# Induced attention and a maxout layer on one core: the first phase's loads, steps and score banks put in another order, and other slots' maxout sums kept in PSUM

## The chip, the core and the metric

The kernel runs on one core of a Trainium2 chip (trn2). Time is device microseconds of one execution, lower is better. The profile is of one execution; its engines are PE (TensorE, matmuls; PEld is its weight load), DVE (VectorE), ACT (ScalarE), POOL (GpSimd) and SP (SyncE, which issues the DMAs). Each engine works through its own queue strictly in the order in which the program wrote it, and waits there on semaphores of the others.

## The reference

Four batches of 12544 tokens with 128 channels first attend from 32 inducing vectors to the tokens (`h`), then from the tokens to `h`; the result goes through a maxout layer of width 768.

```python
def mab(q, kv):
    s = scale * (q @ kv.transpose(0, 2, 1))
    a = np.exp(s - s.max(-1, keepdims=True))
    a /= a.sum(-1, keepdims=True) + 1e-09
    return a @ kv
h = mab(I, x)
y = mab(x, h)                       # 50176 tokens x 128
m = np.maximum(np.maximum(y @ w1, y @ w2), y @ w3)
return (m @ w_out).astype(np.float32)
```

The weights arrive as float64. x is read in float32.

## The kernel before

**Tiling.** A batch has 98 tiles of 128 tokens: group 0 has 2 tiles ("short"), groups 1 to 6 have 16. A full group is four chunks of 512 columns, so a batch has 25 chunks. A chunk needs six slots, one for each 128 of the 768 hidden units: 600 slots in all. A full group's 24 slots are called a window; in this text (b, g) is the window of batch b and group g, and slot k of it is k = 0 to 23.

**First phase** (`phase1_first`, L511, run by the string `STEPS1`). Batch 0's attention from the inducing vectors, and the conversion of the float64 weights, stand in one hand-written order of short steps. `T g.k` transposes four tiles of group g on PE into one of four PSUM banks, `c g.k` copies them out on ACT. `S g` multiplies them with the inducing vectors on PE (into bank `aux0` or `aux1` by turns), `M` takes the maximum on DVE, `D` and `G` spread it over the partitions (ACT, PE), `L` takes the least over the parts (DVE), `E` is the exponential on ACT, `R` a transpose on DVE, `U` the product with the tokens on PE into one bank, `H` the copy of that product to SBUF (ACT). `K` adds the groups up (POOL for groups 0 to 3, DVE for 4 and 5; group 6 is added by `hs`). `W k` is the next step of the conversion of weight k (0 w2, 1 w_out, 2 w1, 3 w3): six operations over 768 columns on DVE, of which the fifth, an addition, is on POOL for w1 and w3, then for w1 one and for w3 two subtractions of w2; `z` is the square of a weight's high half on ACT, which the sixth operation reads. `F n` issues n matmuls whose result nobody reads. `rec`, `hT` form `h` at the end; from there on the first chunks start.

**Loads.** `first_loads` issues the DMAs of the groups of batch 0 (0 to 6) and of the four weights (7 w2, 8 w_out, 9 w1, 10 w3) on SP in the order of `LOADS`.

**The slots** (`advance`, L808, and `stage2`, L889). Step s of the main loop issues for slot s+1 the matmul `pu` (L819) and its Relu on ACT (`ru`, L834), for slot s the matmul `pv` (L825) and the maximum `h = max(pv, ru)` on DVE (L852), for slot s-1 the rounding `hi` of h on ACT (L841) and the rest `lo = h - hi`, on POOL (L849) or, where `low` says so, on DVE at the end of the next step (L855), and for slot s-6 the three matmuls that add hi and lo times w_out into the chunk's bank `acc` (L898). `pu` and `pv` have two banks each, so `pv` of slot s+2 waits for the maximum of slot s. [...] `acc` alternates between two banks (`bank_o`); the one not in use is called `spare`.

**The turns.** Beside the slots, the plan of the main loop puts the attention of the batches 1 to 3 from the inducing vectors into the windows, one group ("turn", L1012 on) at a time: at slot 2 of a window three blocks of matmuls for it, two slots later its maximum (DVE, L407), then two exchanges of partial maxima between partitions by small copies on POOL (`turn_swap`, L429: two copies issued in step 5 and four in step 9), each followed by a reduction on DVE (L437: to `mq` in step 8, to `mm` in step 11), and the exponential. Windows (0,1) to (0,3) have a second such place at slot 14. Windows (2,5), (2,6) and those of batch 3 have no turn. The scores of the next group against `h` are worked on in steps 3 to 15 of a window (DVE L742 to L776).

**Which slots' `lo` is on DVE before.** In batch 3 the slots 0, 5, 14, 18, 21. In (0,1), (0,2) and in group 5 of the other batches 4, 16, 18, 21, all with h in SBUF; in group 6 the same four, 18 and 21 with h in `aux1`; in all other windows 4, 15, 18, 21, the last three with h in `aux1`. So slot 4 of each window of batches 0 to 2 is on DVE, with h in SBUF.

Of the kernel before, what the change touches and what calls it, by code (L numbers as in the profile page):

```python
# [8 lines left out]
F32 = mybir.dt.float32  # L9
# [16 lines left out]
def kernel(ctx, tc, x, xt, ind_t, w1, w2, w3, w_out, out):  # L26
    nc = tc.nc
    B, N, C = x.shape
    M = ind_t.shape[1]
    DF = w1.shape[1]  # L30
    P = 128
    NT = N // P
    NJ = DF // P
# [4 lines left out]
    OB = 2  # L38
    MANUAL = {mybir.EngineType.PE, mybir.EngineType.Activation, mybir.EngineType.SP, mybir.EngineType.DVE, mybir.EngineType.Pool}

    LOADS = (0, 7, 1, 2, 8, 3, 4, 9, 5, 10, 6)
    GROUPS = (0, 1, 2, 3, 4, 5, 6)
    STEPS1 = (
# [8 lines left out]
    )  # L52

    TC = 4
    ORDER = "a a b a a b a b 0 w l a b a a b b 1 2 a b p c b P s X 3 Y S z s s s s s b s"
    STEPS2 = (3, 6, 7, 8, 9, 10, 11, 12, 14, 15)
    scale = 1.0 / float(C) ** 0.5
    LOWVEC = (4, 16, 18, 21)
    LOWBANK = (4, 15, 18, 21)
    LOWLAST = (0, 5, 14, 18, 21)  # L60
    OUTVEC = (0, 2)
    UW = 2 * DF + C
# [3 lines left out]
    groups = []  # L66
    t0 = 0
    while t0 < NT:
        nt = NT % GT if t0 == 0 and NT % GT else GT
# [4 lines left out]
    NG = len(groups)  # L74
# [43 lines left out]
    xts_free = [const.tile([P, GT * P], F32, name=f"xT{i}", tag=f"xT{i}") for i in range(XTB)]  # L118
    xgs_free = [const.tile([P, GT, C], F32, name=f"xg{i}", tag=f"xg{i}") for i in range(XB)]
    w_space = xts_free.pop()  # L120
    shelf = const.tile([P, UW + 2 * groups[0]["nt"] * P + 2 * P + 2 * M + OB * 512 + groups[0]["nt"] * C], F32, name="shelf")
    shelf_at = [0]

    def place(n):
        shelf_at[0] += n
        return shelf[:, shelf_at[0] - n : shelf_at[0]]
# [2 lines left out]
    short_t = [place(groups[0]["nt"] * P) for i in range(2)]  # L129
    short_x = place(groups[0]["nt"] * C).rearrange("p (t c) -> p t c", c=C)  # L130
    iT = place(M)

    def load_raw(src):
        r = bp.tile([P, 2 * DF], U32, name="raw", tag="raw", bufs=4)
# [115 lines left out]
    def start_batch(b):  # L250
        st = state[b] = {"xT": {}, "xg": {}, "a": {}, "s": {}}
        if b == 0:
            st["lst"] = bp.tile([P, NG], F32, name="lst", tag="lst", bufs=1)
            st["mneg"] = bp.tile([P, NG], F32, name="mneg", tag="mneg", bufs=1)
            st["hg"] = outs[1].rearrange("p (g c) -> p g c", c=C)
        else:
            st["mm"] = bp.tile([P, NK], F32, name="mm", tag="mm")
            st["fac"] = bp.tile([P, NK], F32, name="fac", tag="fac")
            st["hs"] = bp.tile([P, C + 1], F32, name="hs", tag="hs")

    def load_tokens(b, k):
        for gi in turns[k]:
# [28 lines left out]
    def attend_products(b, gi, bank):  # L291
        w = groups[gi]["nt"] * M
        st = state[b]
        xT = st["xT"][gi]
        sp = bank
        for q in range(NQ):
            nc.tensor.matmul(
                out=sp[q * M : (q + 1) * M, :w], lhsT=iT, rhs=xT[:, q * w : (q + 1) * w], start=True, stop=True
            )
        st["a"][gi] = sp  # L300
# [210 lines left out]
    def phase1_first():  # L511

        start_batch(0)
        nc.sync.dma_start(out=iT, in_=ind_t)
        nc.scalar.mul(out=iT, in_=iT, mul=scale)
        first_loads()
        st = state[0]
        weights = [convert(k) for k in range(4)]

        groupwise = {  # L520
            "S": lambda gi: attend_products(0, gi, bank_a[GROUPS.index(gi) % 2]),
            "M": lambda gi: attend_max(0, gi),
            "D": lambda gi: attend_column(0, gi),
            "G": lambda gi: attend_spread(0, bank_o[0]),
            "L": lambda gi: attend_least(0, gi),
            "E": lambda gi: attend_weights(0, gi),
            "R": lambda gi: attend_transpose(0, gi),
            "U": lambda gi: attend_sums(0, gi, bank_u[1] if gi == GROUPS[-1] else bank_o[1]),
            "H": lambda gi: attend_keep(0, gi),
            "K": lambda gi: add_group(st, gi),  # L530
            "W": lambda k: next(weights[k], None),
            "z": measure,
            "F": unread_products,
        }
        once = {
            "w2T": transpose_w2,
            "w2h": copy_w2,
            "woh": lambda: nc.scalar.copy(out=wo_hi, in_=wo),
            "least": lambda: combine_least(st),
            "wts": lambda: combine_weights(st),  # L540
            "lw": lambda: sum_groups(st),
            "fac": lambda: last_factor(st),
            "tl": lambda: last_sum(st),
            "tot": lambda: total_sums(st, bank_o[0]),
            "rec": lambda: invert_total(st),
            "hs": lambda: add_last(st),
            "selw": lambda: last_mask(st),
            "pa": lambda: combine_groups(st, "hs", st["selw"], bank_u[0]),
            "sum": lambda: combine_groups(st, "hb", sel[:, :M], bank_u[0]),
            "hT": lambda: combine_states(st, NQ),  # L550
        }
        for step in STEPS1.split():
            if step in once:
                once[step]()
            elif step[0] in "Tc":
                gi, k = step[1:].split(".")
                (transpose_x if step[0] == "T" else copy_x)(0, int(gi), int(k))
            else:
                groupwise[step[0]](int(step[1:]))
        xts_free.append(w_space)  # L560
        start_batch(1)
        load_channels(1, 0)

# [248 lines left out]
    def advance():  # L812

        s = pipe["next"]
        pipe["next"] += 1
        if s + 1 < len(slots):
            c, j = slots[s + 1]
            pu, w = bank_u[(s + 1) % 2], c.w
            nc.tensor.matmul(  # L819
                out=pu[:, :w], lhsT=state[c.b]["us"][:, 2 * j * P : (2 * j + 1) * P], rhs=c.pT[:, :w], start=True, stop=True  # L820
            )
        if 0 <= s < len(slots):
            d, j = slots[s]
            pv = bank_v[s % 2]
            nc.tensor.matmul(  # L825
                out=pv[:, : d.w],
                lhsT=state[d.b]["us"][:, (2 * j + 1) * P : (2 * j + 2) * P],
                rhs=d.pT[:, : d.w],
                start=True,
                stop=True,  # L830
            )
        if s + 1 < len(slots):
            ru = hp.tile([P, 512], F32, name="ru", tag="ru", bufs=3)
            nc.scalar.activation(out=ru[:, :w], in_=pu[:, :w], func=AF.Relu)  # L834
            relus[s + 1] = ru
        low = pipe.pop("low", None)
        if 0 <= s - 1 < len(slots):
            c, j = slots[s - 1]
            h = sums.pop(s - 1)
            hi = hp.tile([P, 512], F32R, name="hi", tag="hi", bufs=9)  # L840
            nc.scalar.copy(out=hi[:, : c.w], in_=h[:, : c.w])  # L841
            lo = hp.tile([P, 512], F32R, name="lo", tag="lo", bufs=10)
            c.hh.append(hi)
            c.hl.append(lo)
            args = dict(out=lo[:, : c.w], in0=h[:, : c.w], in1=hi.bitcast(F32)[:, : c.w])
            if c.low(j):
                pipe["low"] = args
            else:
                nc.gpsimd.tensor_sub(**args)  # L849
        if 0 <= s < len(slots):  # L850
            h = bank_a[1] if d.in_bank(slots[s][1]) else hp.tile([P, 512], F32, name="h", tag="h", bufs=5)
            nc.vector.tensor_max(out=h[:, : d.w], in0=pv[:, : d.w], in1=relus.pop(s)[:, : d.w])  # L852
            sums[s] = h
        if low:
            nc.vector.tensor_sub(**low)  # L855

    class Chunk:
# [8 lines left out]
                self.key = "B" if q else "A"  # L866
                self.base = 0 if q is None else groups[0]["nt"] if q == 0 else (q - 1) * TC

        def low(self, k):

            if self.q is None:
                return False
            if self.b + 1 == B:
                return NJ * self.q + k in LOWLAST
            return NJ * self.q + k in (LOWVEC if self.first_free() > min(LOWBANK[1:]) else LOWBANK)

        def first_free(self):

            if self.b + 1 == B:
                return 0  # L880
            if self.gi == NG - 2 or self.b == 0 and self.gi < 3:
                return WIN
            return 18 if self.gi == NG - 1 else 13

        def in_bank(self, k):

            return self.low(k) and NJ * self.q + k >= self.first_free()

    def stage2(c, j):  # L889
        us = state[c.b]["us"]  # L890
# [260 lines left out]
```

## Time and profile before

| | |
|---|---|
| time, median of 3 runs | 818.93 us (818.26 to 819.09) |
| the profiled execution | 818.5 us |
| its span in the profile | 816.7 us |
| PE busy in the span | 806.1 us (99%) |
| DVE, ACT, POOL busy | 654.7, 719.2, 661.1 us |
| granted TensorE clock | 1.00 |

The page has the busy time of each engine, the span in slices, the DMA queues, the chain of work that ended last, and the costliest groups of instructions by line of the kernel. In rows of the timeline the first two numbers are the start and the duration in us; "x8" is a number of merged instructions, and a bracket at the end of a row tells how long the engine had been idle and what ended it. In rows of groups, "busy us, mean ns" stand behind the count. In rows of waits stand the waiting line, what it waited for, the total in us, the number of waits and the longest.

### The profile page before, as it was taken

The numbers are of one execution on the slowest core, as the hardware profiler recorded it, in microseconds if no ns is written. First come the engines' busy times: TensorE is split into PE (matmuls) and PEld (weight loads), VectorE is DVE, ScalarE is ACT, GpSimd is POOL, SyncE is SP. The second block draws the span as 40 slices with busy tenths as digits, with TensorE's granted clock in tenths as the row PEclk, the third lists the DMA queues.
The fourth block names the chain that finished last, engine by engine and source line by source line (L and its number), as shares of the span: only waits on it lengthen the run. The fifth ranks groups of instructions, "written<-read, shape, count | busy, mean of one in ns | idle before, by whom it ended". The sixth has DMA issues, their size and how long they took to land.

```text
span 816.7 us, 15025 instructions
## 1 busy us (share of the span) xinstructions
PE 806.1 (99%) x4565; PEld 628.3 (77%) x4565; DVE 654.7 (80%) x1198; ACT 719.2 (88%) x1446; POOL 661.1 (81%) x640
## 2 busy tenths in 40 slices
PE   8999999999999999999999999999999999999998
PEld 5667778777787787777777777877778778777886
DVE  6889778787796797887987978878789878878874
ACT  6779889898898898988988989989889999999996
POOL 0369898798798987977988889889878888878886
PEclk9999999999999999999999999999999999999999
DMA  9334643543553335335453353344232222222221
GB/s 344 140 149 141 212 148 106 183 125 105 157 173 123 126 112 175 125 106 177 130 159 117 110 175 120 110 127 126 59 98 66 84 65 78 69 81 74 62 79 51
DMA packets 45408, 101.47 MB, mean 124 GB/s; under 512 B 9360, under 2 KB 15376, under 8 KB 40208
## 3 DMA queue, kind: packets, MB, share of 16 engines
q1 hardware_dynamic: 45184, 100.39, 38.6%
q8 instruction: 36, 0.59, 0.3%
q14 instruction: 44, 0.36, 0.1%
q10 hardware_dynamic: 144, 0.13, 0.0%
HBM read 48.12 MB, written 25.69 MB: 90 GB/s over the span
## 4 chain that ended last, share of the span: by engine, by line
PE 92%; DVE 3%; DMA 2%; ACT 1%; issue 1%; POOL 0%; SPq 0%; DVEq 0%; ACTq 0%
PE acc L898 49%; PE pv L825 16%; PE pu L819 16%; PE aux L707 3%; PE acc L894 3%; PE acc L485 2%; PE aux L388 2%; DMA raw<-in_w_dram 2%; DMA xg<-in_x_dram 1%; POOL rest L207 0%; DVE h L852 0%; ACT ru L834 0%; PE aux L669 0%; DVE mx L745 0%; ACT hi L841 0%
## 5 line engine op out<-in xcount | busy, mean ns | idle before, releaser
L849 POOL TENSOR_TENSOR lo<-h,hi 128x512 fp32r<-128x512 f32 (+1 forms) x498 | 626.6, 1288 | 107.3 <-ACT hi L841 61.8
L852 DVE TENSOR_TENSOR h<-pv,ru 128x512 f32<-128x512 f32 (+1 forms) x534 | 356.2, 672 | 129.6 <-PE pv L825 100.7
L834 ACT ACTIVATE ru<-pu 128x512 f32<-128x512 f32 (+1 forms) x600 | 367.6, 613 | 66.5 <-PE pu L819 62.1
L841 ACT CAST hi<-h 128x512 fp32r<-128x512 f32 (+1 forms) x534 | 333.5, 625 | 4.7 <-DVE h L852 3.6
L898 PE MATMUL acc<-hi,wo_hi 128*128 128x512 f32 (+1 forms) x601 | 235.0, 391 | 0.0
L825 PE MATMUL pv<-pT,us 128*128 128x512 f32 (+1 forms) x600 | 232.7, 388 | 1.6 <-DVE h L852 1.4
L819 PE MATMUL pu<-pT,us 128*128 128x512 f32 (+1 forms) x600 | 231.9, 387 | 0.1
L898 PE MATMUL acc<-hi,wo_lo 128*128 128x512 f32 (+1 forms) x601 | 231.5, 385 | 0.0
L898 PE MATMUL acc<-lo,wo_hi 128*128 128x512 f32 (+1 forms) x601 | 231.3, 385 | 0.0
L898 PEld LDWEIGHTS acc<-hi,wo_hi 128*128 128x128 f32 x601 | 112.8, 188 | 41.5 <-issue 20.5
L825 PEld LDWEIGHTS pv<-pT,us 128*128 128x128 f32 x600 | 112.6, 188 | 29.3 <-DVE h L852 5.4
L819 PEld LDWEIGHTS pu<-pT,us 128*128 128x128 f32 x600 | 112.6, 188 | 24.6 <-ACT ru L834 1.7
L898 PEld LDWEIGHTS acc<-lo,wo_hi 128*128 128x128 f32 x601 | 112.8, 188 | 23.0
L898 PEld LDWEIGHTS acc<-hi,wo_lo 128*128 128x128 f32 x601 | 112.9, 188 | 21.8
L852 DVE TENSOR_TENSOR aux<-pv,ru 128x512 f32<-128x512 f32 x66 | 45.9, 695 | 11.8 <-PE pv L825 5.3
L855 DVE TENSOR_TENSOR lo<-aux,hi 128x512 fp32r<-128x512 f32 x66 | 45.2, 686 | 0.8 <-PE acc L898 0.8
L841 ACT CAST hi<-aux 128x512 fp32r<-128x512 f32 x66 | 41.3, 626 | 0.1
L910 ACT COPY shelf<-acc 128x512 f32<-128x512 f32 (+1 forms) x65 | 39.3, 604 | 0.0
L894 PE MATMUL acc<-pT,us 128*128 128x512 f32 (+1 forms) x100 | 38.8, 388 | 0.0
L855 DVE TENSOR_TENSOR lo<-h,hi 128x512 fp32r<-128x512 f32 x36 | 30.0, 833 | 0.4 <-PE acc L898 0.2
L207 POOL TENSOR_TENSOR rest<-rest,t 128x768 f32<-128x768 f32 x2 | 3.7, 1828 | 28.7 <-DVE rest L203 23.6
L429 POOL COPY mq<-mq 32x1 f32<-32x1 f32 (+2 forms) x108 | 20.4, 188 | 5.2
(166 smaller groups left out, 545.9 us busy)
## 6 DMA issues: line engine op xcount, KB each, us to landing
out_dram<-shelf SPq DMA_DIRECT2D x95, 256.0 KB, 2.0
xg<-in_x_dram SPq DMA_DIRECT2D x22, 1024.0 KB, 5.7
xT<-in_xt_dram SPq DMA_DIRECT2D x18, 1024.0 KB, 5.0
pT<-ph SPq DMA_DIRECT2D x184, 64.0 KB, 2.0
pT<-pl SPq DMA_DIRECT2D x184, 64.0 KB, 2.0
raw<-in_w_dram SPq DMA_DIRECT2D x3, 768.0 KB, 15.0
us<-uh SPq DMA_DIRECT2D x24, 52.0 KB, 2.7
us<-ul SPq DMA_DIRECT2D x24, 52.0 KB, 1.9
```

The costliest lines, as they stand in the source:

```text
L429: nc.gpsimd.tensor_copy(out=far[to : to + step], in_=own[lo : lo + step])
L707: nc.tensor.matmul(out=sp[q * M : (q + 1) * M, :w], lhsT=st["hT"][:, :M], rhs=xT[:, q * w : (q + 1) * w], start=True, stop=True)
L819: nc.tensor.matmul(out=pu[:, :w], lhsT=state[c.b]["us"][:, 2 * j * P : (2 * j + 1) * P], rhs=c.pT[:, :w], start=True, stop=True)
L825: nc.tensor.matmul(out=pv[:, : d.w], lhsT=state[d.b]["us"][:, (2 * j + 1) * P : (2 * j + 2) * P], rhs=d.pT[:, : d.w], start=True, stop=True,)
L834: nc.scalar.activation(out=ru[:, :w], in_=pu[:, :w], func=AF.Relu)
L841: nc.scalar.copy(out=hi[:, : c.w], in_=h[:, : c.w])
L849: nc.gpsimd.tensor_sub(**args)
L852: nc.vector.tensor_max(out=h[:, : d.w], in0=pv[:, : d.w], in1=relus.pop(s)[:, : d.w])
L855: nc.vector.tensor_sub(**low)
L894: nc.tensor.matmul(out=c.acc[:, :w], lhsT=us[:, 2 * DF :], rhs=c.pT[:, :w], start=True, stop=False)
L898: nc.tensor.matmul(out=c.acc[:, cs], lhsT=lhs[:, j, :], rhs=rhs[j][:, cs], start=False, stop=(j == NJ - 1 and rhs is c.hl and cs.stop == w),)
L910: (nc.vector.tensor_copy if by_vector else nc.scalar.copy)(out=o[:, : c.w], in_=c.acc[:, : c.w])
```

## The change

The first phase: w1 is loaded in the place of w_out and w_out in the place of w1; `STEPS1` is a new order of the same steps; the scores of the last group go into the transpose bank `pu0` instead of `aux0`. The slots: `low`, `first_free` and `in_bank` become one function `home`, which reads from tables the slots whose `lo` is on DVE and where their h lies: "h" SBUF, "a" `aux1`, "o" the spare one of the two `acc` banks. The tile `hs` of the later batches lies in a fixed place.

```diff
-    LOADS = (0, 7, 1, 2, 8, 3, 4, 9, 5, 10, 6)
+    LOADS = (0, 7, 1, 2, 9, 3, 4, 8, 5, 10, 6)
...
+        "F4 T0.0 c0.0 F3 S0 W0 M0 F4 T1.0 W0 D0 T1.1 W0 c1.0 W0 T1.2 c1.1 W0 T1.3 c1.2 G0 c1.3 L0 "
+        "z0 F1 S1 W0 T2.0 T2.3 c2.0 M1 T2.2 c2.3 D1 E0 W2 F1 G1 c2.2 T2.1 W2 c2.1 z2 W2 F2 S2 L1 "
+        "W2 E1 T3.2 T3.3 R0 W2 c3.2 M2 T3.1 R1 U0 c3.1 T3.0 D2 c3.3 G2 W2 T4.2 c3.0 T4.3 L2 W2 E2 "
+        "S3 H0 R2 c4.2 U1 M3 T4.1 W1 H1 D3 T4.0 W1 c4.3 U2 c4.0 W1 c4.1 G3 W1 z1 T5.3 T5.1 W1 "
+        "c5.3 T5.0 S4 c5.0 L3 W1 c5.1 T5.2 E3 M4 T6.1 c5.2 W3 T6.0 c6.1 W3 T6.2 H2 D4 T6.3 W3 "
+        "c6.0 S5 c6.3 W3 c6.2 G4 M5 z3 W3 S6 L4 R3 D5 E4 G5 M6 w2T L5 least E5 W3 U3 wts D6 lw K0 "
+        "R4 G6 H3 K1 L6 U4 R5 E6 K2 woh K4 R6 F1 U5 fac K3 w2h tl U6 K5 W3 selw tot F2 hs pa rec "
+        "sum F2 hT W3 "
...
-    LOWVEC = (4, 16, 18, 21)
-    LOWBANK = (4, 15, 18, 21)
+    LOWS = {15: "a", 18: "a", 20: "o", 21: "a"}
+    LOWS_AT = {
+        (0, 1): {4: "h", 16: "h", 20: "o"},
+        (0, 2): {4: "h", 8: "o", 20: "o"},
+        **{(b, 5): {8: "o", 14: "o", 20: "o"} for b in range(3)},
+        **{(b, 6): {14: "o", 18: "a", 20: "o", 21: "a"} for b in range(3)},
+    }
...
+    sums_at = [place(C + 1) for _ in range(2)]
...
-            st["hs"] = bp.tile([P, C + 1], F32, name="hs", tag="hs")
+            st["hs"] = sums_at[b % 2]
...
-            "S": lambda gi: attend_products(0, gi, bank_a[GROUPS.index(gi) % 2]),
+            "S": lambda gi, *half: attend_products(
+                0, gi, bank_u[0] if gi == GROUPS[-1] else bank_a[GROUPS.index(gi) % 2], *half
+            ),
...
-            if c.low(j):
+            if c.home(j):
                 pipe["low"] = args
             else:
                 nc.gpsimd.tensor_sub(**args)
...
-            h = bank_a[1] if d.in_bank(slots[s][1]) else hp.tile([P, 512], F32, name="h", tag="h", bufs=5)
+            home = d.home(slots[s][1])
+            h = {"a": bank_a[1], "o": spare[0]}.get(home)
+            if h is None:
+                h = hp.tile([P, 512], F32, name="h", tag="h", bufs=5)
...
+        def home(self, k):
 
             if self.q is None:
-                return False
...
+                return None
+            lows = dict.fromkeys(LOWLAST, "a") if self.b + 1 == B else LOWS_AT.get((self.b, self.gi), LOWS)
+            return lows.get(NJ * self.q + k)
```

The old order of the steps:

```python
"F4 T0.0 c0.0 F1 S0 M0 D0 F2 G0 W0 z0 W0 T1.0 W0 T1.1 c1.0 L0 W0 E0 T1.2 c1.1 R0 T1.3 W0 "
"c1.2 c1.3 F2 S1 T2.0 M1 T2.1 c2.0 W0 T2.3 D1 c2.1 G1 T2.2 c2.3 L1 W1 U0 c2.2 W1 z1 F1 S2 "
"W1 E1 W1 F2 T3.3 H0 T3.0 W1 c3.3 T3.1 c3.0 T3.2 W1 c3.1 c3.2 R1 woh F2 S3 M2 T4.1 D2 M3 "
"G2 c4.1 W2 T4.0 D3 T4.2 L2 c4.0 W2 G3 E2 T4.3 L3 W2 U1 c4.2 W2 c4.3 E3 T5.1 R2 W2 S4 z2 "
"R3 T5.3 M4 c5.1 T5.2 W2 D4 T5.0 H1 G4 c5.0 W2 U2 c5.2 z3 W3 T6.1 W3 T6.0 c5.3 T6.2 H2 W3 "
"T6.3 c6.1 W3 S5 c6.0 c6.3 L4 W3 U3 E4 M5 D5 R4 c6.2 G5 H3 L5 S6 least W3 wts E5 K0 U4 M6 "
"K1 R5 D6 G6 w2T L6 K2 K4 E6 lw U5 fac K3 R6 w2h U6 tl K5 W3 tot F2 selw hs pa rec sum F2 hT W3 "
```

More of the change, by code (lines that the diff above doesn't have):

```diff
@@ L120 @@
     w_space = xts_free.pop()
-    shelf = const.tile([P, UW + 2 * groups[0]["nt"] * P + 2 * P + 2 * M + OB * 512 + groups[0]["nt"] * C], F32, name="shelf")
+    shelf = const.tile([P, UW + 2 * groups[0]["nt"] * P + 2 * P + 2 * M + OB * 512 + groups[0]["nt"] * C + 2 * (C + 1)], F32, name="shelf")
     shelf_at = [0]
@@ L867, in __init__ @@
                 self.base = 0 if q is None else groups[0]["nt"] if q == 0 else (q - 1) * TC
-        def low(self, k):
+        def home(self, k):
             if self.q is None:
-                return False
[L873 to L887, printed above, removed]
+                return None
+            lows = dict.fromkeys(LOWLAST, "a") if self.b + 1 == B else LOWS_AT.get((self.b, self.gi), LOWS)
+            return lows.get(NJ * self.q + k)
     def stage2(c, j):
```

8 rows, old and new, of the table STEPS1 are left out of this document.

## The prediction, made before the changed kernel was run

> **What bounds the kernel now.** I read the page first: the span, the busy times and the chain of work that ended last.
>
> ```profile
> span 816.7 us, 15025 instructions
> PE 806.1 (99%) x4565; PEld 628.3 (77%) x4565; DVE 654.7 (80%) x1198; ACT 719.2 (88%) x1446; POOL 661.1 (81%) x640
> PE 92%; DVE 3%; DMA 2%; ACT 1%; issue 1%; POOL 0%; SPq 0%; DVEq 0%; ACTq 0%
> ```
>
> Behind the first phase the kernel is a stream of matmuls without gaps, so another engine counts there only where it makes PE wait: taking work from DVE gains nothing by itself, and a delay of DVE costs nothing until a `pv` has to wait for its bank. The first phase (up to some 41 us) ends with a chain of other engines. So I looked at three things: the end of that chain, the few waits of PE in the stream, and how much slack PE has where the change puts more on another engine.
>
> The profiled execution took 818.5 us, 1.8 us more than its span and 0.4 us less than the median of the three runs, 818.93. I make the sum against 818.5 and add the 0.4 us at the end. A measurement of this kernel can tell about 0.2% (1.6 us) from no change.
>
> **First phase: the loads.** Here are the issue of the third place's load (w_out), its time to landing from the view of DMAs, the moment at which DVE got w1, and DVE's longest wait in the phase (timeline).
>
> ```profile
> 4.60 0.46 SPq L136 DMA_DIRECT2D raw<-in_w_out_dram  x1
> raw<-in_w_out_dram SPq DMA_DIRECT2D x1, 768.0 KB, 9.0
> 21.95 0.56 DVE L190 TENSOR_SCALAR t<-raw 128x768 uint32<-128x768 uint32 x1 [0.49 <-DMA raw<-in_w_dram]
> 12.50 0.69 DVE L307 TENSOR_REDUCE mq<-aux 128x1 f32<-128x512 f32 x1 [2.16 <-PE aux L297]
> ```
>
> w_out lands at 13.6 us, w1 at 21.95. Both have 768 KB, nothing else moves on SP, and the loads land in the order of issue; so I take it that w1 now lands at 13.6 and w_out at 21.95. [...]
>
> **First phase: DVE.** Its operations, by form, and the end of the phase: the last transpose `R6` (L351), the product `U6` (L365, from the chain of waits) and `hT`.
>
> ```profile
> L194 DVE SCALAR_TENSOR_TENSOR t<-raw,t 128x768 uint32<-128x768 uint32 x4 | 3.8, 959 | 0.1
> L190 DVE TENSOR_SCALAR t<-raw 128x768 uint32<-128x768 uint32 x4 | 2.2, 556 | 0.6 <-DMA raw<-in_w_dram 0.5
> L207 POOL TENSOR_TENSOR rest<-rest,t 128x768 f32<-128x768 f32 x2 | 3.7, 1828 | 28.7 <-DVE rest L203 23.6 <-DVE mneg L326 5.1
> L307 DVE TENSOR_REDUCE mq<-aux 128x1 f32<-128x512 f32 x6 | 4.1, 682 | 2.2 <-PE aux L297 2.2
> L351 DVE STREAM_TRANSPOSE aT<-a 128x512 f32<-128x512 f32 x6 | 4.1, 700 | 0.6 <-ACT a L337 0.6
> 37.55 0.71 DVE L351 STREAM_TRANSPOSE aT<-a 128x512 f32<-128x512 f32 x1 [0.38 <-ACT a L337]
> 38.32 1.08 PE pu L365 x32
> 40.89 0.29 DVE L634 TENSOR_TENSOR hT<-pu,rec 128x128 f32<-128x128 f32 x1
> ```
>
> The change neither adds nor drops a DVE operation here, so only DVE's idle time can shrink. In the new order DVE does w2 and `M1` before 13.6 and waits there for w1. Then come w1's steps (0.56, 0.96, 0.56, 0.96, then the addition of 1.83 on POOL, beside which DVE does `R0`, `M2` and `R1`, some 1.6, then 0.96 and 0.96), `R2`, `M3`, `L1` and `L2`: 8.3 us, up to 21.9, just when w_out lands. From there to the end of `R6`: w_out 4.9 (two steps of 0.56, four of 0.96), w3's first four 3.0 and its sixth 0.96, `M4` to `M6` 2.0, `R3` to `R6` 2.8, and about 1.5 of small ones (`L3` to `L6`, `least`, `lw`, `K4`). That is 15.2; DVE starts an operation up to 0.1 us before the one ahead of it ends, so I take 14.8, and R6 ends at 36.75 if DVE waits for nothing. It does wait once that I can see: `K4` reads the product `U4`, which PE begins after `R4`, and R4 now stands behind w3's sixth step and M6. U4 (1.08) ends 0.4 us after `R5`; so K4 is late, `U5` behind it starts at 36.6, and `U6` behind U5 at 37.5. Before, U6 started at 38.32. What follows U6 (`tot`, F2, `rec`, `hT`, 2.9 us) is unchanged. **Gain 0.8 us.** If K4 doesn't wait it is 1.5; if `S6` or one of ACT's steps ahead of `M6` comes half a us later than I have it, it is a loss of 0.5. I keep both ends. The bank change of `S6` costs nothing and takes away a wait for `E4`; `hs` in a fixed place costs nothing.
>
> The F-products in front decide little. Here are two pairs of transposes, eight matmuls each:
>
> ```profile
> 7.00 1.97 PE L281 MATMUL pu<-shelf,xg 128*128 128x128 f32 x8
> 12.36 1.09 PE L281 MATMUL pu<-shelf,xg 128*128 128x128 f32 x8
> ```
>
> At 7.0 us PE runs at half of its later speed, at 12.4 no more. F3 and F4 close the gaps of PE from 4.2 us on. If PE gets fast by 9 us, c1.3 and z0 end before 11 and DVE waits for w1 alone; if not, M1 ends at 14.2 and 0.6 of the 0.8 us are lost. [...]
>
> **The stream: what goes.** The subtractions `lo` on DVE by the place of h, one of them, and the `pv` of PE around two such:
>
> ```profile
> L855 DVE TENSOR_TENSOR lo<-aux,hi x66: 673/687/693, 142.0 to 809.0; 128x512 fp32r<-128x512 f32 x66
> L855 DVE TENSOR_TENSOR lo<-h,hi x36: 665/681/1828, 61.5 to 624.6; 128x512 fp32r<-128x512 f32 x36
> 353.72 1.79 DVE L855 TENSOR_TENSOR lo<-h,hi 128x512 fp32r<-128x512 f32 x1
> 354.73 0.39 PE L825 MATMUL pv<-pT,us 128*128 128x512 f32 x1
> 356.77 0.50 PE L825 MATMUL pv<-pT,us 128*128 128x512 f32 x1 [0.74 <-DVE h L852]
> 610.24 0.39 PE L825 MATMUL pv<-pT,us 128*128 128x512 f32 x1
> 612.23 0.50 PE L825 MATMUL pv<-pT,us 128*128 128x512 f32 x1 [0.70 <-DVE h L852]
> ```
>
> From a bank the subtraction never takes over 0.693 us, from SBUF up to 1.83. Twice, at slot 4 of (1,4) and of (2,6), the slow one holds up the maximum and with it PE: the two `pv` lie 2.04 and 1.99 apart where 1.13 is usual. The change leaves three SBUF subtractions, all in (0,1) and (0,2). **Gain 0.9 + 0.9 = 1.8 us**; at least 0 if a bank's subtraction turns out as slow.
>
> **The stream: what comes.** Slot 4's `lo` moves from DVE to POOL in 14 windows, ahead of the copies of the turn on POOL's queue (`lo` of slot 4 is issued at the start of step 5, the first two copies in step 5, the last four in step 9 behind slot 8's `lo`). This is POOL in (0,4), before:
>
> ```profile
> 158.18 1.31 POOL L849 TENSOR_TENSOR lo<-h,hi 128x512 fp32r<-128x512 f32 x1
> 159.42 0.20 POOL L419 COPY mq<-mm 128x1 f32<-128x1 f32 x1
> 159.68 0.40 POOL L429 COPY mq<-mq 64x1 f32<-64x1 f32 x2
> 160.42 5.30 POOL L849 TENSOR_TENSOR lo<-h,hi 128x512 fp32r<-128x512 f32 x4 [0.34 <-PE acc L898]
> 165.78 0.83 POOL L429 COPY mq<-mq 32x1 f32<-32x1 f32 x4
> 166.69 5.07 POOL L849 TENSOR_TENSOR lo<-h,hi 128x512 fp32r<-128x512 f32 x4
> ```
>
> With one more `lo` (1.30 and 0.05 to the next) at 159.68 the two copies run from 161.03 to 161.43 and the four `lo` of slots 5 to 8 from 161.5. Undisturbed by DVE's subtraction they take 5.07 instead of 5.30, up to 166.6; so the four copies end at 167.47 instead of 166.61, **0.86 us later** (1.35 and 0.1 less the idle 0.34 and the 0.23). DVE's queue behind them, and PE:
>
> ```profile
> 166.90 0.15 DVE L437 TENSOR_REDUCE mm<-mq 128x1 f32<-128x3 f32 x1
> 166.96 0.68 DVE L852 TENSOR_TENSOR h<-pv,ru 128x512 f32<-128x512 f32 x1
> 167.56 0.68 DVE L910 COPY shelf<-acc 128x512 f32<-128x512 f32 x1
> 168.16 0.72 DVE L770 STREAM_TRANSPOSE aux<-aux 128x512 f32<-128x512 f32 x1
> 168.78 0.67 DVE L852 TENSOR_TENSOR h<-pv,ru 128x512 f32<-128x512 f32 x1
> 169.63 0.39 PE L825 MATMUL pv<-pT,us 128*128 128x512 f32 x1
> ```
>
> `mm` (L437) reads those copies. It ran 0.28 after them and now waits until 167.49, 0.59 later than before, however early DVE is. Behind it stand the maximum of slot 12, the copy of a finished chunk, a transpose and the maximum of slot 13, without a gap; that one now ends at 170.04 instead of 169.45. `pv` of slot 15 needs its bank. How close it may follow is seen in (1,1), where `mm` waits for the copies already:
>
> ```profile
> 265.89 0.83 POOL L429 COPY mq<-mq 32x1 f32<-32x1 f32 x4
> 266.75 0.16 DVE L437 TENSOR_REDUCE mm<-mq 128x1 f32<-128x3 f32 x1
> 268.67 0.67 DVE L852 TENSOR_TENSOR h<-pv,ru 128x512 f32<-128x512 f32 x1
> 269.39 0.50 PE L825 MATMUL pv<-pT,us 128*128 128x512 f32 x1
> ```
>
> 0.05 us behind the maximum. So in (0,4) `pv` starts at 170.09 instead of 169.63: PE stands **0.46 us**, and nothing gives it back. Nine windows are built like this: (0,4), (0,6), (1,2) to (1,4), (1,6), (2,2) to (2,4); 9 x 0.46 = 4.1. In (1,1) and (2,1) nothing is spare, so some 1.0 of delay less 0.1 that DVE's freed 0.6 us gives back ahead of it: 2 x 0.9 = 1.8. In (0,5) and (1,5) slot 8 went to DVE, so the copies are early, but its subtraction lies in front of `mm`: 0.28 later less the 0.13 spare at `pv` is 0.15 each, 0.3. In (0,1) to (0,3) PE has a block of the second turn at slot 14, which hides it; (2,5) and (2,6) have no turn. **Loss 6.2 us**; bounds 3.2 (0.25 in each of the nine, 0.5 in the two) and 8 (0.6 and 1.1).
>
> Slot 20's h in the spare `acc` bank: written in step 20, read by DVE last at the end of step 22; the next chunk's first matmul into that bank comes in step 24, over 0.6 us later. Its copy out was issued in step 18. So 0; at slots 14 and 8 it is closer, up to 0.1 in a few windows, within the bounds. Five fewer subtractions on DVE are hidden under PE; five more on POOL cost only through the copies.
>
> **Sum.** 818.5 - 0.8 - 1.8 + 6.2 = 822.1; with the 0.4 of the median 822.5 us. This case alone: 819.5 to 825.
>
> **The rivals.** *The copies' delay doesn't reach PE.* It needs 0.28 us of slack at `mm`, 0.13 at `pv` and the idle and slow time on POOL (0.57), together about 1.0, to hold the added 1.45; so if the added `lo` with its changeovers costs under 1.0 us, or DVE's queue between `mm` and slot 13 loses one operation, nothing is lost. Then 818.93 - 0.8 - 1.8 = 816.3, faster. Against it: no 128x512 `lo` on POOL in these rows takes under 1.25 us. For it: DVE is 0.6 us earlier ahead of `mm`, which I count as useless. *Half the copies' delay*: the parts nearly cancel, 818.9 + 6.2 / 2 - 1.8 - 0.8 = 819.4. For it: each wait is a fraction of a us, and PE, once late, has slack for the next. Against it: the nine windows are far apart. *The slow subtraction is chance and not the place of h*: the 1.8 stay, 824.3. [...]
>
> **How the numbers follow.** The forecast gets 0.55, and with the 1.8 kept 0.07 more; the first rival 0.24; the second 0.14. Faster than 817.3 is nearly all of the first rival: 0.23. Within 0.2% lie the second rival but a third, 0.04 of the forecast and a little of the first: 0.17. Slower 0.60. The range must reach the first rival: 815.8 to 824.8.
>
> **What will show it.** DVE's `mm` (L437) idle before it with POOL as the releaser in most windows with a turn; waits of PE's `pv` for DVE's h, one in each of eleven windows, 0.3 to 1 us each; no subtraction L855 over 0.7 us but at slots 4 and 16 of the first two windows; `hT` near 40.1 us instead of 40.89. If `hT` comes later than 41, or `pv` has no such waits, I am wrong.

## The result, and the profile after

The changed kernel takes 823.08 us (median of 4 runs, 822.85 to 823.47), the kernel before on the same chip 818.89 (818.26 to 819.09); the ratio is 1.0053, 95% interval 1.0035 to 1.007. The forecast was 822.5. The span of the profiled execution grew from 816.7 to 821.3 us. Two executions of the runs below, one of the kernel before and one with the copies late, ran at a granted clock of 0.66 and took some 1147 us; they are left out of every comparison.

From the page of the profile after: the span, the busy times, and the chain that ended last by engine.

```profile
span 821.3 us, 15084 instructions
PE 808.4 (98%) x4567; PEld 628.1 (76%) x4567; DVE 649.3 (79%) x1193; ACT 720.7 (88%) x1446; POOL 657.3 (80%) x645
PE 82%; DVE 5%; ACT 3%; POOL 3%; issue 3%; DMA 2%; SPq 1%; POOLq 0%; DVEq 0%; ACTq 0%
```

PE's share of the chain fell from 92 to 82%, and POOL, which stood at 0, holds 3%: the path to the end now goes again and again through POOL and DVE, although both are less busy than before. In the changed kernel's lines, POOL's `lo` is L857 (849 before), DVE's `lo` L866 (855), the maximum L863 (852), `pv` L833 (825), the copies of the turn L425 and L435 (419, 429), their reduction `mm` L443 (437).

The view of the waits of the kernel after: the waiting line, what it waited for, us in total, times, longest. In the stream the first row stood at 1.4 us in 2 waits before, the second at 0.5 in 1.

```profile
PE pv L833 <- DVE h L863: 4.0, 13, 0.5
DVE mm L443 <- POOL mq L435: 6.8, 12, 1.3
```

The timeline of window (0,4) of the kernel after, POOL, then DVE, then PE (its `pv` of slots 14 to 16), and the same three `pv` before:

```profile
159.10 1.29 POOL L857 TENSOR_TENSOR lo<-h,hi 128x512 fp32r<-128x512 f32 x1
160.45 0.40 POOL L435 COPY mq<-mq 64x1 f32<-64x1 f32 x2
160.93 5.05 POOL L857 TENSOR_TENSOR lo<-h,hi 128x512 fp32r<-128x512 f32 x4
166.05 0.83 POOL L435 COPY mq<-mq 32x1 f32<-32x1 f32 x4
166.91 0.16 DVE L443 TENSOR_REDUCE mm<-mq 128x1 f32<-128x3 f32 x1 [0.39 <-POOL mq L435]
166.99 0.69 DVE L863 TENSOR_TENSOR h<-pv,ru 128x512 f32<-128x512 f32 x1
167.60 0.68 DVE L908 COPY shelf<-acc 128x512 f32<-128x512 f32 x1
168.20 0.72 DVE L778 STREAM_TRANSPOSE aux<-aux 128x512 f32<-128x512 f32 x1
168.83 0.67 DVE L863 TENSOR_TENSOR h<-pv,ru 128x512 f32<-128x512 f32 x1
168.03 0.39 PE L833 MATMUL pv<-pT,us 128*128 128x512 f32 x1
169.55 0.50 PE L833 MATMUL pv<-pT,us 128*128 128x512 f32 x1 [0.22 <-DVE h L863]
170.81 0.39 PE L833 MATMUL pv<-pT,us 128*128 128x512 f32 x1
```

```profile
168.50 0.39 PE L825 MATMUL pv<-pT,us 128*128 128x512 f32 x1
169.63 0.39 PE L825 MATMUL pv<-pT,us 128*128 128x512 f32 x1
170.77 0.39 PE L825 MATMUL pv<-pT,us 128*128 128x512 f32 x1
```

Slot 4's `lo` (159.10) now stands between the first copy and the next two, and four more stand ahead of the last four copies. They end at 166.88, `mm` has waited 0.39 for them, DVE then works without a gap up to the maximum of slot 13, and `pv` of slot 15 starts 0.05 behind its end. From slot 14 to 15 lie 1.52 us instead of 1.13, from 15 to 16 1.26 instead of 1.14: 0.51 us lost.

Put side by side like this, slot by slot, the starts of the same `pv` in both traces give the balance:

| where | forecast, us | measured, us |
|---|---|---|
| first phase (first `pv`) | -0.8 | -0.72 |
| stalls behind slow subtractions, (1,4) and (2,6) | -1.8 | -1.1 - 1.5 = -2.6 |
| the nine windows | +4.1 | +4.9 (0.44 to 0.55 each, (1,2) 0.87) |
| (1,1), (2,1) | +1.8 | +1.8 |
| (0,5), (1,5) | +0.3 | +0.7 |
| (0,2), (2,5) | 0 | +0.4 |
| sum | +3.6 | +4.6 |

### The profile page after: what moved, and what is told of

The parts are those of the page before. It is cut to its first block, busy times and chain, and to the rows that moved or that the text cites. A ratio compares the mean times of both kernels' runs of the same rounds, so it can differ in the third digit from the quotient of the medians.

```text
span 821.3 us, 15084 instructions
## 1 busy us (share of the span) xinstructions
PE 808.4 (98%) x4567; PEld 628.1 (76%) x4567; DVE 649.3 (79%) x1193; ACT 720.7 (88%) x1446; POOL 657.3 (80%) x645
## 4 chain that ended last, share of the span: by engine, by line
PE 82%; DVE 5%; ACT 3%; POOL 3%; issue 3%; DMA 2%; SPq 1%; POOLq 0%; DVEq 0%; ACTq 0%
PE acc L896 43%; PE pv L833 14%; PE pu L827 14%; PE aux L715 3%; DVE h L863 2%; PE acc L892 2%; POOL lo L857 2%; PE aux L394 2%; PE acc L491 2%; DMA xT<-in_x_dram 2%; ACT ru L842 1%; DVE shelf L908 1%; ACT hi L849 1%; POOL mq L435 1%; SPq L109 1%
## 5 line engine op out<-in xcount | busy, mean ns | idle before, releaser
L857 POOL TENSOR_TENSOR lo<-h,hi 128x512 fp32r<-128x512 f32 (+1 forms) x503 | 625.1, 1273 | 115.9 <-ACT hi L849 60.2
L863 DVE TENSOR_TENSOR h<-pv,ru 128x512 f32<-128x512 f32 (+1 forms) x506 | 338.2, 672 | 129.8 <-PE pv L833 98.9
L849 ACT CAST hi<-h 128x512 fp32r<-128x512 f32 (+1 forms) x506 | 313.5, 620 | 2.2 <-DVE h L863 1.1
L833 PE MATMUL pv<-pT,us 128*128 128x512 f32 (+1 forms) x600 | 233.6, 389 | 4.1 <-DVE h L863 4.0
L833 PEld LDWEIGHTS pv<-pT,us 128*128 128x128 f32 x600 | 112.6, 188 | 33.9 <-DVE h L863 10.5
L863 DVE TENSOR_TENSOR aux<-pv,ru 128x512 f32<-128x512 f32 x66 | 45.9, 695 | 10.3 <-PE pv L833 4.0
L866 DVE TENSOR_TENSOR lo<-aux,hi 128x512 fp32r<-128x512 f32 x66 | 45.3, 686 | 0.0
L863 DVE TENSOR_TENSOR acc<-pv,ru 128x512 f32<-128x512 f32 x28 | 19.4, 694 | 6.8 <-PE pv L833 5.4
L715 PE MATMUL aux<-xT,hT 128*32 128x512 f32 x184 | 24.5, 605 | 0.0
```

Of the source, the lines that this page charges most:

```text
L715: nc.tensor.matmul(out=sp[q * M : (q + 1) * M, :w], lhsT=st["hT"][:, :M], rhs=xT[:, q * w : (q + 1) * w], start=True, stop=True)
L833: nc.tensor.matmul(out=pv[:, : d.w], lhsT=state[d.b]["us"][:, (2 * j + 1) * P : (2 * j + 2) * P], rhs=d.pT[:, : d.w], start=True, stop=True,)
```

## The experiments

Three theories were open after this. *The copies*: slot 4's `lo` ahead of the last copies makes the loss. *The bank*: h in the spare `acc` bank holds something up. *The phase*: the new first phase matters more, or in another direction, than the 0.7 us in the pair of traces. All ratios are to the kernel before on the same chip.

**The first phase alone**: the new loads, steps and score bank with the old slots.

```diff
-    LOWS = {15: "a", 18: "a", 20: "o", 21: "a"}
+    LOWS = {4: "h", 15: "a", 18: "a", 21: "a"}
...
-        (0, 1): {4: "h", 16: "h", 20: "o"},
+        (0, 1): {4: "h", 16: "h", 18: "h", 21: "h"},
...
```

> New loads, new order of steps and S6 in the transpose bank, with the old slots on DVE. My theory: the first phase ends 0.7 us earlier (hT at 40.17 instead of 40.89) and the stream is that of the kernel before: 818.89 - 0.7 = 818.2 us, ratio 0.999. Rival, that the loss comes from what the first phase hands on (other load times, banks): near 823, ratio 1.005.

Measured 816.58 us (816.31 to 817.18, 11 runs), ratio 0.9979 [0.997, 0.9988]: 1.8 us faster than before, a miss of 1.6 us. Slot by slot its trace is only 0.48 us ahead at the first `pv`; another 1.13 come in window (1,4), where the slow subtraction of the trace before isn't there, though no slot was changed.

**The slots alone**: the new tables with the old loads, steps and score bank.

```diff
-    LOADS = (0, 7, 1, 2, 9, 3, 4, 8, 5, 10, 6)
+    LOADS = (0, 7, 1, 2, 8, 3, 4, 9, 5, 10, 6)
...
```

> The old first phase with the new slots on DVE and the new places of h. My theory: the whole loss without the gain of the first phase, 823.08 + 0.7 = 823.8 us, ratio 1.006. Rival (first phase to blame): 818 to 819.

Measured 823.49 us (823.23 to 824.13, 5 runs), ratio 1.0062 [1.0049, 1.0076]. PE's waits are those of the changed kernel to the digit (4.0 us, 13 times). So the loss belongs to the slots. The whole new phase is worth 0.4 us by the times (823.49 less 823.08) and 0.9 when each is counted against the kernel before on its own chip (5.1 and 4.2 us more); that is hardly more than the spread of the runs, and it isn't settled more closely than this.

**The copies ahead**: the changed kernel with the last four copies issued one step earlier, ahead of slot 8's `lo`.

```diff
-        at(s + 7, turn_swap, b, k, M)
+        at(s + 6, turn_swap, b, k, M)
```

> The changed kernel, only the four copies of a turn's second exchange are issued one step earlier, so that they stand on POOL's queue ahead of the lo of slot 8 and end 1.26 us earlier. My theory (mm waits for the copies and PE for what stands behind mm): the waits in the nine windows (0.44 to 0.87 us each, 4.9 in sum) and in (1,1), (2,1) (1.28 each) go, those of (0,5), (1,5) stay: 823.1 - 4.9 - 2.6 = 815.6 us, ratio 0.996. Rival A (h in the spare acc bank holds up PE): no change, 823. Rival B (POOL's five more subtractions as such): no change, 823.

Measured 816.07 us (815.78 to 816.45, 6 runs), ratio 0.9972 [0.996, 0.9983], 7.0 us less than the changed kernel (6.5 when each is counted against the kernel before on its own chip). The waits of PE's `pv` for DVE's h are gone, and the timeline of (0,4) of this kernel, which starts 0.58 later here than in the trace after, shows why:

```profile
161.53 3.81 POOL L857 TENSOR_TENSOR lo<-h,hi 128x512 fp32r<-128x512 f32 x3
165.40 0.83 POOL L435 COPY mq<-mq 32x1 f32<-32x1 f32 x4
167.01 0.15 DVE L443 TENSOR_REDUCE mm<-mq 128x1 f32<-128x3 f32 x1
```

The copies end at 166.23, DVE comes to `mm` at 167.01 and nothing waits. The nine windows are back at their old length or shorter; in (0,5), (1,5), (0,2) and (2,5) 0.53, 0.35, 0.27 and 0.21 us are still lost.

**The copies ahead in the kernel before**, the control for it: the same edit at L974 of the kernel before.

> The kernel before with the last four copies one slot earlier, the control for e3. If the copies hold up TensorE only because slot 4's subtraction was put ahead of them, it gives the 0.35 of (1,1) and of (2,1) and nothing in the nine windows: 817.7 us, ratio 0.999. If earlier copies are a gain of their own (6 to 7 us as between e3 and the changed kernel), 812. A slow subtraction that falls out with the new timing would take 1 or 2 us more: 815.7 to 816.7.

Measured 815.75 us (815.6 to 815.84, 5 runs), ratio 0.9965 [0.9952, 0.9979]. Of the nine windows six stayed within 0.05, (1,6) and (2,3) became 0.11 and 0.23 longer; 0.5 came ahead of the first `pv`, where this kernel has the old phase unchanged, and 1.1 and 1.5 in (1,4) and (2,6), where the slow subtractions fell out; the total is the lower end of what I had put down for that case. The 0.35 that I expected in each of (1,1) and (2,1) didn't come (0.09 shorter and 0.05 longer): it stands in the traces of the kernels in which slot 4's `lo` has left DVE (0.35 and 0.33 with the copies ahead), so it belongs to that and not to the copies. So earlier copies are no gain of their own: they pay only where slot 4's `lo` stands ahead of them.

**Slot 4 back on DVE**, with the rest of the change kept.

```diff
-    LOWS = {15: "a", 18: "a", 20: "o", 21: "a"}
+    LOWS = {4: "h", 15: "a", 18: "a", 20: "o", 21: "a"}
...
-        **{(b, 5): {8: "o", 14: "o", 20: "o"} for b in range(3)},
+        **{(b, 5): {4: "h", 14: "o", 20: "o"} for b in range(3)},
-        **{(b, 6): {14: "o", 18: "a", 20: "o", 21: "a"} for b in range(3)},
+        **{(b, 6): {4: "h", 14: "o", 18: "a", 20: "o", 21: "a"} for b in range(3)},
```

> The changed kernel, only slot 4's lo is back on DVE with h in SBUF in the 14 windows (in group 5 instead of slot 8); the slots 14 and 20 keep h in the spare acc bank. My theory: the copies end as before, all those waits go, 823.1 - 4.9 - 2.6 - 0.7 = 814.9 us, and up to two or three slow subtractions from SBUF come back at 0.9 us each: 814.9 to 817.5, ratio 0.995 to 0.998. Rival A (the spare acc bank): stays near 823.

These are 16 windows; the 14 of the text above are those with a turn. Measured 816.64 us (816.11 to 817.19, 11 runs), ratio 0.9977 [0.9968, 0.9985]. The loss is gone although the copies are issued in the same step as in the change, so it is the one subtraction ahead of them. One slow subtraction is back, at slot 4 of (2,6). DVE's subtractions of this kernel by where h lies (duration in ns: least, median, most):

```profile
L866 DVE TENSOR_TENSOR lo<-aux,hi x66: 677/692/693, 141.9 to 807.4; 128x512 fp32r<-128x512 f32 x66
L866 DVE TENSOR_TENSOR lo<-acc,hi x25: 673/682/692, 81.5 to 627.9; 128x512 fp32r<-128x512 f32 x25
L866 DVE TENSOR_TENSOR lo<-h,hi x19: 668/683/1828, 61.1 to 608.0; 128x512 fp32r<-128x512 f32 x19
```

25 subtractions from the spare `acc` bank, none above 0.692 us, and with these banks in use the loss is gone: the theory of the bank falls.

**The copies late**: one step later than in the change, behind slot 9's `lo`.

```diff
-        at(s + 7, turn_swap, b, k, M)
+        at(s + 8, turn_swap, b, k, M)
```

> The changed kernel with the last four copies of the turn one slot later on GpSimd's queue, behind one more subtraction (1.25 us by the profile of after). If their place sets the wait, each of the eleven windows that waits already loses another 1.0 to 1.25 us and the two windows (0,5) and (1,5) about 0.9: 823.1 + 11 x 1.15 + 1.8 = 837 us, ratio to before 1.022; bounds 833 to 842. If half of a delay is taken up by slack behind the first late step, 830. If the copies don't set the wait, 823.

Measured 841.66 to 843.11 us (3 runs), ratio 1.0289 [1.0273, 1.0305]: the direction is that of the theory, the size some 5 us above it.

> The kernel of e5_copies_late once more, for its trace by windows, which the first time was taken at a granted clock of 0.656. Its time was 842.4, that is 19.3 more than the changed kernel. If the copies' place alone makes it, the nine windows that lost 0.5 each lose 1.6 to 1.9 each, (1,1) and (2,1) 2.1, (0,5) and (1,5) 1.2 to 1.6, and windows that lost nothing in the changed kernel, (0,1) to (0,3), now lose the rest, some 1 us each; (2,5) and (2,6), which have no turn, lose nothing. If the loss lies elsewhere (in (2,5), (2,6) or the last stage too), it isn't the copies.

841.32 us (2 runs, 842.47 and 840.17; the profile is of the first), ratio 1.0279 [1.0256, 1.0301]. PE's waits in this kernel's stream, and its `pv` of slots 14 to 16 of (1,1):

```profile
PE pv L833 <- DVE h L863: 16.1, 23, 1.7
275.53 0.50 PE L833 MATMUL pv<-pT,us 128*128 128x512 f32 x1 [1.73 <-DVE h L863]
277.34 0.80 PE L833 MATMUL pv<-pT,us 128*128 128x512 f32 x1 [0.36 <-DVE h L863]
279.64 0.63 PE L833 MATMUL pv<-pT,us 128*128 128x512 f32 x1
```

Against the trace after, each of the nine windows and (0,3) lost 1.23 to 1.27 us more: one `lo` of POOL with its changeover, whole, so there is no slack left in them. (1,1) and (2,1) lost 2.66 each, and only 1.26 of it is a longer wait, in front of slot 14 (slot 15 waited 0.36 in the kernel after too, slot 16 waits for nothing). The other 1.40 is PE's clock: in this execution the granted clock is 0.50 from 277.0 to 280.4 us and from 481.8 to 485.2, 3.4 us each time, and the matmuls there start 0.43 us apart instead of 0.23. These are the two places where PE had stood longest (1.73 and some 0.37 us, close together); after the waits of 0.8 to 1.2 us elsewhere the clock stays at 1.00. The other execution, 2.3 us shorter, has a mean clock of 1.000, so the slow clock seems to come and go. (0,1) lost 0.4, (0,2) 0.6, (0,5) and (1,5) 0.35; (2,5) and (2,6), without a turn, nothing. What my 837 had too low is this clock in (1,1) and (2,1), 2.8 us, and (0,1) to (0,3), 2.3 us, which I had as covered.

**Slot 8 too**: the copies ahead, and slot 8's `lo` back on POOL.

```diff
-        (0, 2): {4: "h", 8: "o", 20: "o"},
-        **{(b, 5): {8: "o", 14: "o", 20: "o"} for b in range(3)},
+        (0, 2): {4: "h", 20: "o"},
+        **{(b, 5): {14: "o", 20: "o"} for b in range(3)},
...
```

> The changed kernel with the last four copies one slot earlier (as in e3) and slot 8's subtraction back on GpSimd in (0,2), (0,5), (1,5), (2,5). If what is left in e3 in these windows (0.27, 0.53, 0.35 and 0.21 us by its trace) comes from slot 8's subtraction in front of the maximum of the turn, it goes: 816.07 - 1.4 = 814.7 us, ratio 0.995. If GpSimd's extra subtraction delays the copies there all the same, it stays: 816.0.

Measured 814.11 us (813.88 to 814.38, 5 runs), ratio 0.9947 [0.9934, 0.9959]. All four windows are within 0.03 us of their old length or shorter. Slot 8's subtraction on DVE, 0.7 us in front of `mm`, was what cost them. Of the 2.0 us between the two kernels the windows make 1.5; the rest is the first `pv`, 0.44 us earlier in this trace with the phase unchanged.

**R4 earlier**: the kernel of the last run with `R4` ahead of w3's sixth step.

```diff
-        "c6.0 S5 c6.3 W3 c6.2 G4 M5 z3 W3 S6 L4 R3 D5 E4 G5 M6 w2T L5 least E5 W3 U3 wts D6 lw K0 "
-        "R4 G6 H3 K1 L6 U4 R5 E6 K2 woh K4 R6 F1 U5 fac K3 w2h tl U6 K5 W3 selw tot F2 hs pa rec "
+        "c6.0 S5 c6.3 W3 c6.2 G4 M5 z3 W3 S6 L4 R3 D5 E4 G5 M6 w2T L5 least R4 E5 W3 U3 wts D6 lw K0 "
+        "G6 H3 K1 L6 U4 R5 E6 K2 woh K4 R6 F1 U5 fac K3 w2h tl U6 K5 W3 selw tot F2 hs pa rec "
```

> e6 with the first phase's transposition R4 ahead of the last but one step of w3, so that U4 and with it K4 don't hold up VectorE at 36.3 us (0.63 idle there in the profile of after). If VectorE's queue sets the end of the phase, hT ends 0.4 to 0.6 earlier than in e6 and the time is 814.2 us. If the phase ends by other things (the landing of the loads, w3's steps), hT and the time stay within 0.2 of e6.

Measured 813.79 us (813.64 to 814.32, 5 runs), ratio 0.9944 [0.9931, 0.9956]; the fastest of all, though 0.32 us below the last run is inside the spread of the two. `K4` on DVE, in the kernel after and in this one:

```profile
36.33 0.35 DVE L588 TENSOR_SCALAR shelf<-acc,w 128x128 f32<-128x128 f32 x1 [0.63 <-PE acc L371]
```

```profile
35.79 0.35 DVE L588 TENSOR_SCALAR shelf<-acc,w 128x128 f32<-128x128 f32 x1 [0.16 <-PE acc L371]
39.63 0.29 DVE L642 TENSOR_TENSOR hT<-pu,rec 128x128 f32<-128x128 f32 x1
```

`hT` comes at 39.63; counted from DVE's first step of w1, 25.86 us later instead of 26.75 in the last run (26.64 in the kernel after).

**The loads back in the old order**, under the new steps (the `LOADS` line as above).

> The changed kernel with the old order of the loads (w_out second, w1 last but one) under the new order of steps. The steps take w1 second, and on VectorE everything of group 1 stands behind its conversion. If the order of the loads is tied to the order of the steps, w1's first step waits until it lands at about 21.5 us instead of 13.5, hT comes near 47 us instead of 40.2 and the time is 830 us. If VectorE has enough slack later to take it up, 824 to 826.

Measured 831.49 us (2 runs), ratio 1.0159 [1.0137, 1.0181]. DVE in this kernel:

```profile
20.87 0.56 DVE L196 TENSOR_SCALAR t<-raw 128x768 uint32<-128x768 uint32 x1 [7.48 <-DMA raw<-in_w_dram]
48.46 0.29 DVE L642 TENSOR_TENSOR hT<-pu,rec 128x128 f32<-128x128 f32 x1
```

DVE waits 7.48 us for w1 and begins with it 7.34 us later than in the kernel after, and all of that ends up in `hT` (8.3 later) and in the time (8.4 more). The other 0.95 comes behind that beginning: PE idles 6.08 us up to 24.22, the granted clock is 0.50 from 23.0 to 29.9 us, and eight transpositions there take 1.95 us instead of 1.04. That the slow PE makes the 0.95 is likely, but no run separates it.

**The fillers as few as before**, in the new order.

```diff
-        "F4 T0.0 c0.0 F3 S0 W0 M0 F4 T1.0 W0 D0 T1.1 W0 c1.0 W0 T1.2 c1.1 W0 T1.3 c1.2 G0 c1.3 L0 "
+        "F4 T0.0 c0.0 F1 S0 W0 M0 F2 T1.0 W0 D0 T1.1 W0 c1.0 W0 T1.2 c1.1 W0 T1.3 c1.2 G0 c1.3 L0 "
```

> The changed kernel with the filler products at the start as few as before (F1 and F2 in the place of F3 and F4). If TensorE's clock needs the filled gaps, the first eight transpositions run slowly (1.5 us for eight and not 1.3) until 12 us, M1 ends some 0.6 later and hT with it: 823.7 us. If the early clock doesn't matter, because VectorE waits for the loads anyway, 823.1 and hT at 40.2 +- 0.3.

Median 823.5 us (823.34 to 825.57, 4 runs), ratio 1.0061 [1.0045, 1.0076]; the highest, 825.57, is the profiled execution. Because it lay so far from the other three, it was run again.

> The kernel of e8_fewer_fill once more. Its profiled execution took 825.57 with hT at 42.4 us and a TensorE that was slow until 14.2 us, its three others 823.3 to 823.6. If fewer fillers make the start uncertain and not simply slower, this profile shows hT somewhere between 40.2 and 42.4, with the time following: 823.2 + (hT - 40.3) for the profiled execution, and a median of 823.2 to 823.8.

823.76 us (823.09 to 825.62, 4 runs), ratio 1.007 [1.0052, 1.0089]; the profiled one took 823.51. The same instructions in the two profiles, PE's second block of eight transpositions and the first large scores (`S1`), then `hT`:

```profile
8.87 1.91 PE L287 MATMUL pv<-shelf,xg 128*128 128x128 f32 x8
11.87 1.94 PE L303 MATMUL aux<-xT,shelf 128*32 128x512 f32 x8
42.41 0.29 DVE L642 TENSOR_TENSOR hT<-pu,rec 128x128 f32<-128x128 f32 x1
```

```profile
8.69 1.97 PE L287 MATMUL pv<-shelf,xg 128*128 128x128 f32 x8
11.55 1.06 PE L303 MATMUL aux<-xT,shelf 128*32 128x512 f32 x8
40.50 0.29 DVE L642 TENSOR_TENSOR hT<-pu,rec 128x128 f32<-128x128 f32 x1
```

In one execution PE still works at half speed at 11.9 us (`S1` takes 1.94; it goes on to 15.3), in the other it doesn't (1.06); between the two lie 1.9 us in `hT` and 2.06 in the time. In both the first transposition starts at 3.96; the first block of eight starts at 7.11 in the one and at 6.89 in the other, so at most 0.2 us of the difference was there before. Two of these eight executions took 825.6 us. With the fillers of the change none of the 4 runs was above 823.47, and in the four other kernels with the same first phase (alone, the copies ahead, slot 4 back, slot 8 too) none of 33 lies more than 0.6 us above its kernel's median. So the fillers buy little in the median (0.4 to 0.9 us) and seem to keep out the late start.

## Why the prediction was right

**The loads**: right for w1, whose first step waits for the load and starts at 13.53 (13.6 forecast). w_out lands at 20.79, 1.2 before the forecast 21.95; its first step starts at 21.91 all the same, because DVE's own steps last until then, as the 8.3 us of the forecast have it. The old loads under the new steps show that the two orders belong together.

**DVE's chain and `K4`**: right in mechanism, not established in size. `K4` waits for `U4` as forecast, U6 starts at 37.63 (37.5 forecast), `hT` comes at 40.17 (40.1). But the 40.89 of before, against which I counted the gain of 0.8, is one draw. The unchanged old order gave 40.35 (slots alone) and 40.4 (copies ahead in the kernel before), the unchanged new one 40.00 to 40.71 in six profiles (the kernel after, the first phase alone, the copies ahead, slot 4 back, slot 8 too, the copies late). The runs of the two orders with the same slots say 0.4 to 0.9 us. What the new order does obey: `hT` comes 26.55 to 26.79 us after DVE begins with w1 in all six, and that beginning wanders from 13.45 to 13.95 with the landing of the load and the end of `M1`.

**The clock**: the 0.8 counts on PE being fast by 9 us; that the filled gaps make it so was an assumption that no run had shown. The condition was met in this trace. In the kernel after, PE's second block of eight transpositions takes 1.32 us with a short wait for its tokens in it, the later ones 1.04; single transpositions start 0.21 us apart until 7.95 and 0.11 apart from 8.11 on, so PE is fast by about 8 us. It isn't always: with the same first phase it stays slow until 10.0 (the first phase alone, where the block from 8.97 takes 1.74) and 10.2 (the copies ahead, 1.61 from 9.39), and there DVE doesn't wait for w1 but begins with it when `M1` is done, at 13.66 and 13.95. With fewer fillers the same block takes 1.91 and 1.97. I had weighed a delay of 0.6 us; it can be 1.9.

```profile
8.50 1.32 PE L287 MATMUL pv<-shelf,xg 128*128 128x128 f32 x8
12.44 1.04 PE L287 MATMUL pv<-shelf,xg 128*128 128x128 f32 x8
```

The two runs with fewer fillers show that the moment of the switch differs with nothing changed: the same program turned fast in time for `S1` in one (1.06 us, from 11.55) and only at 15.3 us in the other. What sets that moment no run shows.

**The slow subtractions**: the direction right, the size 0.8 too small, the cause sharper than I had it. In the kernel after no subtraction on DVE is above 0.693 us. The gain was 2.6, because in (2,6) slots 20 and 21 gave 0.37 more, behind the slow one of slot 16, and (1,4) and (2,6) 1.0 to 1.1 each instead of 0.9. But the place of h is only half of it; the other half is who starts first. (1,4) in the kernel before, DVE and POOL, and then the same window in the kernel before with the copies ahead:

```profile
353.72 1.79 DVE L855 TENSOR_TENSOR lo<-h,hi 128x512 fp32r<-128x512 f32 x1
353.67 2.98 POOL L849 TENSOR_TENSOR lo<-h,hi 128x512 fp32r<-128x512 f32 x2 [0.35 <-PE acc L898]
```

```profile
352.57 0.68 DVE L855 TENSOR_TENSOR lo<-h,hi 128x512 fp32r<-128x512 f32 x1
352.88 4.05 POOL L849 TENSOR_TENSOR lo<-h,hi 128x512 fp32r<-128x512 f32 x3 [0.34 <-PE acc L898]
```

POOL ahead by 0.05: DVE takes 1.79. DVE ahead by 0.31: DVE takes 0.68, and POOL's three take 4.05 instead of 3.81. That rival (*the slow subtraction is chance*) was therefore half right: with h in SBUF nearly each of these subtractions meets one of POOL (34 of 36 in the kernel before), and a few tenths of a us, at times hundredths, decide, from run to run, which of the two is held up. This is why the first phase alone and the control gained 1.1 and 2.6 us without a change in these slots.

**The copies**: right, the main term. Forecast for the nine windows 0.46 each, measured 0.44 to 0.55 in eight of them. (1,1) and (2,1) lost 0.91 each, forecast 0.9, but that agreement is luck: in front of slots 14 and 15 they lost 1.28 and 1.30, not 1.0, and at slots 9 and 10 the subtraction that left DVE gave back 0.33 and 0.31, not 0.1. The copies ahead, slot 4 back on DVE and the copies late (each a further `lo`, a further 1.25) confirm it from three sides, and both rivals, that the delay doesn't reach PE and that half of it does, fall with them. The step was too small by 1.7 us in all: `pv` of slot 16 is late too (0.13 in (0,4), on top of 0.38 at slot 15), which I left out; (1,2) lost 0.87, where DVE behind `mm` stood another 0.28 for a `pv`, which I didn't follow up and which comes and goes (0.85 and 0.87 with fewer fillers, but 0.55 with the slots alone and 0.50 with the old loads); and slot 8's subtraction in front of `mm` cost 0.35 and not 0.15 in (0,5) and (1,5), and 0.2 each in (0,2) and (2,5), which I had at nothing. This excess of 1.7 and the 0.8 by which the slow subtractions were too small make the 1.0 us between +3.6 and +4.6 (with 0.1 from the phase). That the time still came within 0.6 us of the forecast is in part luck: these two errors have opposite signs, and the 0.4 that I added for the median helped, because the profiled execution before had been that much below it, and the one after wasn't.

**The spare bank, freed DVE time**: right. No subtraction from it is slow, and 0.6 us of DVE freed ahead of a wait are worth nothing, as slot 4 in the nine windows shows; only in (1,1) and (2,1) they gave the 0.3 above.

## What to carry to other kernels

When work moves to an engine that is less busy, look for the small operations in that engine's queue that somebody waits for; four copies of 0.2 us set the time here, and issuing them one step earlier turned a loss of 4 us into a gain of 2. Then ask what stands ahead of the waiting reduction on its own engine, since an operation put there costs whatever of its length the slack doesn't cover (0.2 to 0.5 of 0.7 us for slot 8). And take the gain of a short phase from several traces, not from one pair: here its end wandered by 0.5 to 0.7 us with nothing changed.

## What the runs showed of the hardware that was not expected

In the trace of the kernel before, a DVE subtraction with both inputs in SBUF and a POOL one that met ran one after the other, not side by side, 34 times of 34. When POOL started 0.02, 0.05 and 0.16 us ahead (slot 4 of (2,6), of (1,4), and at 238.49), DVE took 1.83, 1.79 and 1.68 us instead of 0.68; when DVE started 0.15, 0.31 and 0.40 ahead (at 401.62, 160.11 and 209.48), POOL took 1.68, 1.53 and 1.44 instead of 1.30. So the loser ended its own length less 0.13 to 0.15 us after the winner's end.

In the kernel before and with fewer fillers the granted clock reads 1.00 throughout the first phase, also where eight transpositions take 1.97 us and not 1.04. Whether PE is fast at the start is read from such rows and not from that column. Later slow stretches do stand in the column: 0.50 from 23.0 to 29.9 us with the loads in the old order, where PE had waited 6.08 us up to 24.22, and 0.50 for 3.4 us after each of the two waits of 1.73 us with the copies late. In that execution nearly as much was lost again behind each of these two waits: 1.73 us waited, then 1.40 lost to the slow clock. What makes the clock fall there, and not after the shorter waits, no run shows.
